# A Fourier mixer followed by hash routing: routing in two parts, scatters paced by stage 2, tables in three parts

## The chip, the cores and the metric

The kernel runs on one core of one Trainium2 chip. The metric is the device time of one execution in microseconds. A core has five engines with their own instruction streams: TensorE (PE; its weight loads are shown as PEld), VectorE (DVE), ScalarE (ACT), GpSimd (POOL) and SyncE (SP). Here SP and ACT start ordinary DMA transfers, and POOL starts transfers by descriptors made in software, above all indirect ones (scatter and gather by an index). Each engine runs its instructions in program order, so an instruction that waits holds up all behind it on that engine.

## What is computed

The input x has 8 batches of 2496 tokens with 256 channels. Each channel goes through a real Fourier transform over the tokens, is multiplied by a complex filter, and is transformed back. The result is read as 19968 tokens, and each token goes to one of eight experts, chosen by its id, which is a two-layer network with ReLU (256 to 1024 to 256):

```python
X = np.fft.rfft(x, axis=1)
y = np.fft.irfft(X * (filt_r + 1j * filt_i)[None], n=x.shape[1], axis=1)
x = y.reshape(B * S, D)
expert_idx = token_ids * np.int64(2654435761) % np.int64(E)
for e in range(E):
    mask = expert_idx == e
    out[mask] = np.maximum(x[mask] @ w1[e], 0.0) @ w2[e]
```

All arithmetic is in 32-bit floats.

## The kernel before

**The mixer.** The transform of length 2496 is done as 39 by 64. Per batch there are three stages. Stage 1 (`stage1`, PSUM tile pa) multiplies x tiles by a table of 39-point transforms; ACT copies the result to t1, and ACT's queue stores it to a DRAM buffer d1. Stage 2 (`stage2`, eleven steps: `forward` of step u and `back` of step u - 1) reads d1 in another layout as tiles t2 (`load2`, five loads per batch), multiplies by the table d_t (pb), applies the filter on DVE (y and z: four operations per step), multiplies by the transposed table e_t (pc), and stores through ACT to a DRAM buffer d2. Stage 3 (`stage3`, six pieces) reads d2 as tiles t4 (`load4`), multiplies by the inverse table (pd), copies to o and stores to `mixed` in DRAM (`store3`). For batches 0 and 1 the copy to o is on ACT, for the others on DVE. There are two buffers of o, two of t1, four of t2.

**The routing.** `count`, `route` and `places` (lines 407 to 495) work out on DVE, for every token, its row in `lists`, so that each expert's tokens fill tiles of 128. `listed` scatters token numbers into `lists` with indirect DMAs on POOL, 128 tokens each: 39 scatters for the tokens of each of the four routing stages (batches 0 and 1, 2 and 3, 4 and 5, 6 and 7). `blanks` computes the unused rows and marks them with 7 scatters more. `tile_experts` and `experts` work out which expert each of the 163 tiles belongs to.

**The tables.** `load_tables` loads d_t and the filter in two parts: entries 0 to 7 through SP, 8 to 19 through POOL as soon as the second x tile is there (line 358). `spread_filters` copies the filter to other partitions (DVE and ACT), and `way_back` transposes d_t into e_t on TensorE.

**The experts.** For each of 163 tiles: `load` reads a list (SP) and gathers its rows of mixed (POOL), `turn` transposes them on TensorE (xps, xt), `up` does the first layer (ups) and `down` the second (dps), and the result is scattered to the output (POOL). Weights are loaded when a tile's expert differs. `load` runs four tiles ahead. A tile of a routing stage may be gathered only when its two batches are mixed.

**The order** is written out by hand: `todo` (lines 583 to 605) is a list of pieces, each with a due time. Pieces below zero are issued first, in order of their times; the rest are issued between `up` and `down` of the expert tile whose number is their time. So the opening, before the first expert tile, holds stages 1 to 3 of batches 0 and 1, stage 1 of batch 2 and the first routing stage. A load's due time is put a few steps ahead of its use, but not before the argument `ready`.

Of the kernel before, what the change touches and what calls it, by code (L numbers as in the profile page):

```python
# [11 lines left out]
F32 = mybir.dt.float32  # L12
I32 = mybir.dt.int32
AF = mybir.ActivationFunctionType
OP = mybir.AluOpType
AX = mybir.AxisListType
# [3 lines left out]
P = 128  # L20
B, S, C = 8, 2496, 256
N = B * S
E, F = 8, 1024
# [6 lines left out]
NS, NQ = N1 // 2 + 1, 64  # L30
# [6 lines left out]
NU = (HN + XG) // XG  # L37
# [6 lines left out]
TB = 128  # L44
NT = (N + E * (TB - 1)) // TB
LW = 16
NJ = N // (4 * P)
DP = C // P
FP = F // P
STAGES = (2, 4, 6, 8)  # L50
G = len(STAGES)
NPAD = NT * TB - N
NQP = NPAD // P

# [53 lines left out]
def kernel(  # L108
# [39 lines left out]

    ident = keep.tile([P, P], F32)
    slots = keep.tile([P, G, NJ], I32)  # L150
    number = keep.tile([P, NJ, LW], I32)
    chunk_i = keep.tile([1, 2, NT], I32)
    wf_t = cpool.tile([NR, NK], F32)
# [5 lines left out]
    class Batch:  # L159
# [119 lines left out]
        def stage3(self, u):  # L279

            o = opool.tile([NR, XG, C], F32, name=f"o_{self.b}_{u}", tag="o")
            v, half = divmod(u, XL // XG)

            copy = nc.scalar.copy if self.b < 2 else nc.vector.tensor_copy
            self.products(wi_t, (NK, 2 * NS), N1, self.t4[v][:, half * XG:half * XG + XG, :], o, copy, u, "pd")

            last, self.o = self.o, (o, u)
            if last and self.b >= 2:
                self.store3(*last)
            if self.b < 2 or u == NU - 1:  # L290
                self.store3(o, u)

        def store3(self, o, u):
# [17 lines left out]
    def listed(g, j0, j1):  # L311

        if j0 == 0:
            nc.gpsimd.iota(number[:], pattern=[[1, NJ], [0, LW]], base=P * NJ * g, channel_multiplier=NJ)
        for j in range(j0, j1):
            scatter(number[:, j, :], slots[:, g, j:j + 1], f"lists_{g}")

    batches = [Batch(b) for b in range(B)]

# [28 lines left out]
    rt = rpool.tile([P, 2 + NQP], F32)  # L348
    nc.scalar.dma_start(out=rt[:], in_=r_dram.ap())

    S_PARTS = (slice(0, 8), slice(8, NS))

    def load_tables(part):
        sl = S_PARTS[part]
        eng = nc.sync if part == 0 else nc.gpsimd
        if part:

            nc.gpsimd.tensor_copy(junk[:], batches[0].x[1][0:1, 0, 0:1])
        eng.dma_start(out=d_t[:, sl, :], in_=d_dram.ap()[:, sl, :])
        for k in range(2):  # L360
            load_filter(k, sl, eng)
# [45 lines left out]
    def count():  # L407
# [1 line left out]
        eid_i = slots[:].rearrange("p g j -> p (g j)")  # L409
        nc.vector.tensor_scalar(eid_i, tok[:].rearrange("p g j two -> p (g j) two")[:, :, 0], E - 1, None,  # L410
                                op0=OP.bitwise_and)
        eid = rpool.tile([P, G * NJ], F32)
        nc.vector.tensor_copy(eid[:], eid_i)
        mask = rpool.tile([P, E, G * NJ], F32)
        nc.vector.tensor_tensor(mask[:], eid[:].unsqueeze(1).to_broadcast([P, E, G * NJ]),
                                iota_e[:].unsqueeze(2).to_broadcast([P, E, G * NJ]), op=OP.is_equal)
        maskf = mask[:].rearrange("p e j -> p (e j)")
        run = rpool.tile([P, E * G, NJ], F32)
# [14 lines left out]
    def route():  # L433
# [1 line left out]


        upto = rpool.tile([P, G, E], F32)
        made_in = ps[:, 0, 0:E * G].rearrange("p (e g) -> p g e", g=G)
        nc.vector.tensor_copy(upto[:, 0, :], made_in[:, 0, :])
        for g in range(1, G):  # L440
            nc.vector.tensor_tensor(upto[:, g, :], upto[:, g - 1, :], made_in[:, g, :], op=OP.add)
        full_i = rpool.tile([P, G, E], I32)
        nc.vector.tensor_copy(full_i[:], upto[:])
        nc.vector.tensor_scalar(full_i[:, G - 1, :], upto[:, G - 1, :], float(TB - 1), None, op0=OP.add)
# [27 lines left out]
        nc.vector.tensor_scalar(off0[:], off[:, 0, :], -1.0, None, op0=OP.add)  # L472
        thr = rpool.tile([P, G, E], F32)
        nc.vector.tensor_scalar(thr[:], full[:, 0:G, :], float(TB), 1.0, op0=OP.mult, op1=OP.add)
        acc = rpool.tile([P, E, G * NJ], F32)
        tmp = mask
        nc.vector.tensor_tensor(run[:], run[:], base[:].rearrange("p e g -> p (e g)").unsqueeze(2)
                                .to_broadcast([P, E * G, NJ]), op=OP.add)
        run = run[:].rearrange("p (e g) j -> p e (g j)", g=G)
        nc.vector.tensor_tensor(run, run, mask[:], op=OP.mult)  # L480
        for e in range(E):
            nc.vector.scalar_tensor_tensor(acc[:, e, :], mask[:, e, :], off0[:, e:e + 1], run[:, e, :],
                                           op0=OP.mult, op1=OP.add)
        for g in range(1, G):
            for e in range(E):
                nc.vector.tensor_scalar(tmp[:, e, :], run[:, e, :], thr[:, g, e:e + 1], step[:, g, e:e + 1],
                                        op0=OP.is_ge, op1=OP.mult)
            nc.vector.tensor_tensor(acc[:], acc[:], tmp[:], op=OP.add)

        rv.update(acc=acc, upto=upto, full_t=full_t, made=made, first=first, last=last)  # L490

    def places():
        slot = rv["eid"]
        nc.vector.tensor_reduce(slot[:], rv["acc"][:].rearrange("p e j -> p j e"), axis=AX.X, op=OP.add)
        nc.vector.tensor_copy(slots[:].rearrange("p g j -> p (g j)"), slot[:])

    def tile_experts():
        last = rv["last"]
# [13 lines left out]
    def blanks():  # L512
# [18 lines left out]
        nc.vector.tensor_tensor(at[:], at[:], index, op=OP.add)  # L531
        nc.vector.scalar_tensor_tensor(at[:], first[:, G - 1, 0:1].to_broadcast([P, NQP]), float(TB), at[:],
                                       op0=OP.mult, op1=OP.add)
        at_i = rpool.tile([P, NQP], I32)
        nc.vector.tensor_copy(at_i[:], at[:])
        blank = rpool.tile([P, LW], I32)
        nc.gpsimd.memset(blank[:], N)
        for q in range(NQP):
            scatter(blank[:], at_i[:, q:q + 1], "lists_pad")

    def experts():
        seg = rv["seg"]
# [14 lines left out]
    def spaced(t0, t1, n):  # L557
        return [t0 + (t1 - t0) * u / n for u in range(n)]
# [21 lines left out]
    N_2 = NS // 2 + 1  # L580


    todo = part1(0, spaced(-155, -143, NU)) + [(-152.5, count), (-152.4, route), (-152.3, places)]
    todo += [(-154.9, lambda: load_tables(0)), (-154.8, lambda: load_tables(1))]
    todo += [(t, lambda k=k: way_back(k)) for k, t in enumerate([-142.7, -142.5, -122, -121.8, -121.6])]
    todo += [(-141, lambda: spread_filters(0)), (-125, lambda: spread_filters(1))]
    todo += part2(0, spaced(-131, -101, N_2), -138)
    todo += part1(1, spaced(-129, -105, NU), [-150, -149, -136])
    todo += [(-140, tile_experts), (-130, experts), (-60, blanks)]
    todo += [(-142, lambda: listed(0, 0, NJ))]  # L590
    todo += [(-110, lambda: nc.sync.dma_start(out=wi_t[:], in_=wi_dram.ap()))]
    todo += [(-82 + .1 * i, lambda i=i: (weights(i, 0), weights(i, 1))) for i in range(2)]
    todo += part2(1, spaced(-100, -70, N_2), -103) + part3(0, spaced(-92, -73, NU), -97)
    todo += part1(2, spaced(-70, -60, NU), [-104, -103.9, -78]) + part3(1, spaced(-59.5, -48, NU), -66)

    todo += part1(3, spaced(2, 7, NU)) + part1(4, spaced(15, 20.5, NU))
    todo += part1(5, spaced(21, 27, NU)) + part1(6, spaced(36, 46, NU)) + part1(7, spaced(50, 60, NU))
    todo += part2(2, spaced(.1, 7.4, N_2), -40) + part2(3, spaced(8.5, 15.5, N_2), 7)
    todo += part2(4, spaced(22, 31, N_2), 20.5) + part2(5, spaced(31.2, 46, N_2), 28)
    todo += part2(6, spaced(48, 62, N_2), 47) + part2(7, spaced(63.2, 80, N_2), 61)  # L600
    todo += part3(2, spaced(8, 14, NU), 7.5) + part3(3, spaced(17, 25, NU), 15.6)
    todo += part3(4, spaced(33, 44, NU), 31.5) + part3(5, spaced(49, 63, NU), 46.5)
    todo += part3(6, spaced(67, 83, NU), 62) + part3(7, spaced(84, 101, NU), 81)
    for g, (t0, t1) in enumerate([(1, 23), (30, 62), (70, 102)]):
        todo += [(t, lambda g=g, j=j: listed(g + 1, j, j + 1)) for j, t in enumerate(spaced(t0, t1, NJ))]
    todo.sort(key=lambda t: t[0])
    pre = [t for t in todo if t[0] < 0]
    main = [t for t in todo if t[0] >= 0]
# [11 lines left out]
    def load(i):  # L620

        g = stage_of[i]
        if i % 2 == 0:
            n = min(2, NT - i)
            lst[i] = gath.tile([P, 2, LW], I32, name=f"lst_{i}", tag="lst")
            step = tiles[i + 1] - tiles[i] if n == 2 else 1
            ld = nc.sync.dma_start(
                out=lst[i][:, 0:n, :],
                in_=bass.AP(tensor=lists[:].tensor, offset=lists[:].offset + tiles[i] * TB * LW,
                            ap=[[LW, P], [step * TB * LW, n], [1, LW]]))  # L630
            for later in range(g + 1, G):
                tc.declare_no_dep(ld.ins, group=f"lists_{later}", reason="the tiles of a stage hold tokens of its batches alone")
            tc.add_to_no_dep_group("lists_read", ld.ins)
        xg[i] = gath.tile([P, C], F32, name=f"xg_{i}", tag="xg")
        rows = N + 1 if g == G - 1 else STAGES[g] * S
# [42 lines left out]
        tc.add_to_no_dep_group("out_rows", st.ins)  # L678
        del xg[i]

    for i in range(4):
        load(i)
    turn(0)
    for i in range(NT):
        ht = work.tile([P, FP, TB], F32, name=f"ht_{i}", tag="ht")
        if i + 4 < NT:
            load(i + 4)
        up(i, ht)
        weights(i + 2, 0)
        if i + 1 < NT:  # L690
            turn(i + 1)
        while main and main[0][0] < i + 1:
            main.pop(0)[1]()
        down(i, ht)
        weights(i + 2, 1)
# [29 lines left out]
```

## Time and profile before

| | |
|---|---|
| time | 1719.93 us, median of 3 runs (1709.46 to 1722.15) |
| span of the profiled execution | 1715.1 us |
| TensorE busy, granted clock | 1538.2 us, 0.947 |
| DVE, ACT, POOL busy | 534.9, 216.8, 508.9 us |
| moved by DMA | 257.70 MB, mean 150 GB/s |
| first expert matmul (line 658) | 247.67 us after the start |

The profile is one execution. Busy shares are means over the whole span; the opening of some 248 us and the rest have different limits, so the views by stretches of time are the ones to read. In a listing by time, a line gives start, duration, engine, line of the kernel, operation, tiles written and read, and in brackets how long the engine stood idle before and what ended that wait.

### The profile page before, as it was taken

To read this page: it belongs to the slowest core of one execution; us is meant where nothing else is said; L and a number is where in the kernel's file an instruction comes from. 1 tells how busy PE (TensorE), PEld (TensorE's weight loads), DVE (VectorE), ACT (ScalarE), POOL (GpSimd) and SP (SyncE) were. 2 spreads that over 40 slices of the span, in tenths; PEclk is the share of its full clock that TensorE was granted. 3 is DMA by queue.
4 is the path that set the end of the run, shared out by engine and by line. 5 is a ranking of instruction groups with operands and counts; after the bars stand their busy time and mean duration, and the time that the engine had idled before them with its cause. 6 is when DMAs were issued, how large, how long until landed. Compare 5 with 4: busy or idle time off the path is not lost.

```text
span 1715.1 us, 27107 instructions
## 1 busy us (share of the span) xinstructions
PE 1538.2 (90%) x9522; PEld 1388.9 (81%) x9522; DVE 534.9 (31%) x970; ACT 216.8 (13%) x371; POOL 508.9 (30%) x515
## 2 busy tenths in 40 slices
PE   3266659989997999999999999999999999999997
PEld 2154438867886899989888999899899999999997
DVE  6155104345223444423332444122222122221121
ACT  2031211101111111111110101000000000000000
POOL 2710113322322133433333233344332222222221
PEclk7577769989998999999999999999999999999999
DMA  8378555665766488366554664443426222222220
GB/s 240 111 239 228 149 169 158 196 156 166 209 193 191 126 261 254 112 200 168 148 190 127 191 203 135 128 146 85 158 64 210 88 88 87 87 86 85 85 81 12
DMA packets 160868, 257.70 MB, mean 150 GB/s; under 512 B 38817, under 2 KB 121412, under 8 KB 158733
## 3 DMA queue, kind: packets, MB, share of 16 engines
q1 hardware_dynamic: 102833, 143.67, 28.1%
q10 hardware_dynamic: 35484, 62.57, 11.7%
q0 software_dynamic: 22416, 49.74, 9.5%
q8 instruction: 76, 1.25, 0.3%
q14 instruction: 59, 0.48, 0.1%
HBM read 431.77 MB, written 85.09 MB: 301 GB/s over the span
## 4 chain that ended last, share of the span: by engine, by line
PE 82%; DMA 7%; issue 4%; DVE 3%; another core or an unknown queue 2%; ACT 1%; SPq 1%; ACTq 0%; POOL 0%; POOLq 0%; DVEq 0%
PE ups L658 33%; PE dps L670 32%; PE pd L198 4%; PE pc L258 4%; PE pa L198 4%; PE pb L235 3%; DMA d<-t 2%; DMA t<-d 2%; PE xps L647 2%; DVE z L245 1%; DMA mixed<-o 1%; DMA d<-g 1%; DVE y L242 1%; PE pd L193 0%
## 5 line engine op out<-in xcount | busy, mean ns | idle before, releaser
L658 PEld LDWEIGHTS ups<-xt,w 128*128 128x128 f32 x5216 | 610.8, 193 | 9.4 <-DVE xt L649 1.1
L658 PE MATMUL ups<-xt,w 128*128 128x128 f32 x5216 | 611.6, 276 | 0.7 <-DVE xt L649 0.7
L670 PE MATMUL dps<-w,ht 128*128 128x256 f32 x2608 | 596.6, 382 | 5.8 <-DMA w<-in_moe_w_dram 4.7
L670 PEld LDWEIGHTS dps<-w,ht 128*128 128x128 f32 x2608 | 492.6, 192 | 73.1 <-DMA w<-in_moe_w_dram 5.1
L674 POOL DMA_INDIRECT out_dram<-osb,lst x163 | 161.8, 993 | 628.3 <-DVE osb L673 603.7
L636 POOL DMA_INDIRECT xg<-mixed,lst x163 | 173.3, 1063 | 387.7 <-DMA lst<-lists 140.1
L664 DVE TENSOR_SCALAR ht<-ups 128x512 f32<-128x512 f32 x163 | 112.8, 692 | 556.2 <-PE ups L658 422.3
L662 ACT ACTIVATE ht<-ups 128x512 f32<-128x512 f32 x163 | 97.3, 597 | 1042.4 <-PE ups L658 602.8
L673 DVE COPY osb<-dps 128x256 f32<-128x256 f32 x163 | 69.2, 425 | 399.7 <-PE dps L670 392.8
L304 POOL DMA_INDIRECT lists<-number,slots x156 | 155.6, 997 | 72.2 <-issue 47.0
L258 PE MATMUL pc<-y,e_t 128*128 128x256 f32 x320 | 92.3, 414 | 49.6 <-DVE z L245 28.2
L258 PEld LDWEIGHTS pc<-y,e_t 128*128 128x128 f32 x320 | 63.5, 205 | 67.9 <-issue 53.2
L245 DVE TENSOR_TENSOR z<-pb,filt 64x512 f32<-64x512 f32 x160 | 110.2, 689 | 2.2
L235 PE MATMUL pb<-t,d_t 128*128 128x256 f32 x320 | 89.6, 406 | 20.2 <-DMA t<-d 17.7
L198 PE MATMUL pd<-t,wi_t 120*117 120x256 f32 x320 | 87.9, 422 | 17.2 <-DMA t<-d 7.6
L242 DVE TENSOR_TENSOR y<-pb,filt 128x512 f32<-128x512 f32 x80 | 55.2, 690 | 113.8 <-PE pb L235 62.6
L198 PEld LDWEIGHTS pd<-t,wi_t 120*117 120x117 f32 x320 | 62.2, 203 | 33.9 <-ACT o L200 6.1
L235 PEld LDWEIGHTS pb<-t,d_t 128*128 128x128 f32 x320 | 61.8, 203 | 33.4 <-issue 22.5
L649 DVE COPY xt<-xps 128x256 f32<-128x256 f32 x163 | 67.7, 415 | 57.9 <-PE xps L647 56.5
L261 ACT COPY g<-pc 128x512 f32<-128x512 f32 x80 | 46.7, 586 | 258.1 <-PE pc L258 175.0
L198 PE MATMUL pa<-x,wf_t 117*120 117x256 f32 x264 | 64.9, 393 | 7.2 <-DMA x<-in_x_dram 7.2
L647 PE MATMUL xps<-ident,xg 128*128 128x128 f32 x326 | 62.5, 274 | 7.1 <-DMA xg<-mixed,lst 7.1
(102 smaller groups left out, 390.5 us busy)
## 6 DMA issues: line engine op xcount, KB each, us to landing
w<-in_moe_w_dram SPq DMA_DIRECT2D x322, 1024.0 KB
t<-d SPq DMA_DIRECT2D x80, 256.0 KB
d<-g ACTq DMA_DIRECT2D x80, 256.0 KB
mixed<-o ACTq DMA_DIRECT2D x120, 156.0 KB
d<-t ACTq DMA_DIRECT2D x16, 960.0 KB
t<-d SPq DMA_DIRECT2D x16, 960.0 KB
x<-in_x_dram SPq DMA_DIRECT2D x39, 312.0 KB
x<-in_x_dram SPq DMA_DIRECT2D x21, 234.0 KB
```

The lines of the kernel that those rows point to most:

```text
L198: nc.tensor.matmul(out=ps[0:cols * H, k, :], lhsT=w[:], rhs=src[:, 2 * i + k, :], start=True, stop=True)
L235: nc.tensor.matmul(out=ps[:, i, :], lhsT=d_t[:, s, :], rhs=self.t2[s // SG][:, s % SG, :], start=True, stop=True)
L245: nc.vector.tensor_tensor(out=z[b], in0=ps[a], in1=f_t[1][a, sl, :], op=OP.mult)
L258: nc.tensor.matmul(out=ps[:, i, :], lhsT=e_t[:, 2 * u + i, :], rhs=pr[:, i, :], start=True, stop=True)
L304: st = nc.gpsimd.indirect_dma_start(out=lists[:], out_offset=bass.IndirectOffsetOnAxis(ap=index, axis=0), in_=rows, in_offset=None, bounds ...
L636: ld = nc.gpsimd.indirect_dma_start(out=xg[i][:], out_offset=None, in_=mixed[0:rows, :], in_offset=bass.IndirectOffsetOnAxis(ap=lst[i // 2 ...
L647: nc.tensor.transpose(out=ps[:, dp, :], in_=xg[i][:, dp * P:(dp + 1) * P], identity=ident[:])
L658: nc.tensor.matmul(out=ps[:, k, :], lhsT=w1[:, dp, fp * P:(fp + 1) * P], rhs=xt[i][:, dp, :], start=(dp == 0), stop=(dp == DP - 1))
L662: nc.scalar.activation(out=dst, in_=ps[:], func=AF.Relu)
L664: nc.vector.tensor_scalar_max(dst, ps[:], 0.0)
L670: nc.tensor.matmul(out=ps[:], lhsT=ht[:, fp, :], rhs=w2[:, fp, :], start=(fp == 0), stop=(fp == FP - 1))
L674: st = nc.gpsimd.indirect_dma_start(out=out[:], out_offset=bass.IndirectOffsetOnAxis(ap=lst[i // 2 * 2][:, i % 2, 0:1], axis=0), in_=o[:], ...
```

## The change

It works on the opening, and a little on the expert part.

- The routing is done in two parts. `places(0, 1)` works out the rows of the first routing stage alone, before stage 2 of batch 0; `places(1, G)` does the other three after stage 2 of batch 1. Operations over single experts become operations over all eight.
- The 39 scatters of the first routing stage are issued in pairs, one pair after each step of stage 2 of batches 0 and 1. Each pair reads its rows from a tile `place`, into which DVE copies them at that point of its own order, so that a pair can't start before DVE has come there.
- The tables are loaded in three parts: entries 0 to 7 and 8 to 11 through SP at the start, 12 to 19 through POOL once the first t2 tile of batch 0 is there (`behind`).
- The x loads of batch 1 are placed between the t2 loads of batch 0, and stage 1 of batch 1 runs in the second half of stage 2 of batch 0.
- In stage 3 of batches 0 and 1, a piece's store is issued after the next piece's copies, as for the other batches.
- The seven scatters of blanks move to the times of expert tiles 62 to 69. Some due times in the expert part change a little. Near the end of a routing stage, `load` runs two tiles ahead instead of four.

The diff, cut to its core:

```diff
-            if last and self.b >= 2:
+            if last:
                 self.store3(*last)
-            if self.b < 2 or u == NU - 1:
+            if u == NU - 1:
                 self.store3(o, u)
...
+        index = slots[:, g, :]
+        if g == 0:
+            nc.vector.tensor_copy(place[:, j0:j1], index[:, j0:j1])
+            index = place
         for j in range(j0, j1):
-            scatter(number[:, j, :], slots[:, g, j:j + 1], f"lists_{g}")
+            scatter(number[:, j, :], index[:, j:j + 1], f"lists_{g}")
...
-    S_PARTS = (slice(0, 8), slice(8, NS))
+    S_PARTS = (slice(0, 8), slice(8, 12), slice(12, NS))
+    def behind(ap):
+        nc.gpsimd.tensor_copy(junk[:], ap)
     def load_tables(part):
-        eng = nc.sync if part == 0 else nc.gpsimd
-        if part:
-            nc.gpsimd.tensor_copy(junk[:], batches[0].x[1][0:1, 0, 0:1])
+        eng = nc.sync if part < 2 else nc.gpsimd
...
+    def places(g0, g1):
+        nc.vector.tensor_tensor(run, run, rv["base"][:, :, g0:g1].unsqueeze(3).to_broadcast([P, E, n, NJ]), op=OP.add)
+        nc.vector.tensor_tensor(run, run, mask, op=OP.mult)
+        nc.vector.tensor_tensor(acc, mask, each(rv["off"][:]), op=OP.mult)
+        nc.vector.tensor_tensor(acc, acc, run, op=OP.add)
         for g in range(1, G):
-            for e in range(E):
-                nc.vector.tensor_scalar(tmp[:, e, :], run[:, e, :], thr[:, g, e:e + 1], step[:, g, e:e + 1],
-                                        op0=OP.is_ge, op1=OP.mult)
-            nc.vector.tensor_tensor(acc[:], acc[:], tmp[:], op=OP.add)
+            nc.vector.tensor_tensor(mask, run, each(rv["thr"][:, g, :]), op=OP.is_ge)
+            nc.vector.tensor_tensor(mask, mask, each(rv["step"][:, g, :]), op=OP.mult)
+            nc.vector.tensor_tensor(acc, acc, mask, op=OP.add)
...
-    todo = part1(0, spaced(-155, -143, NU)) + [(-152.5, count), (-152.4, route), (-152.3, places)]
+    todo = part1(0, spaced(-155, -143, NU)) + [(-152.5, count), (-152.4, route), (-142.95, lambda: places(0, 1))]
     todo += [(-154.9, lambda: load_tables(0)), (-154.8, lambda: load_tables(1))]
-    todo += part2(0, spaced(-131, -101, N_2), -138)
-    todo += part1(1, spaced(-129, -105, NU), [-150, -149, -136])
-    todo += [(-140, tile_experts), (-130, experts), (-60, blanks)]
-    todo += [(-142, lambda: listed(0, 0, NJ))]
+    todo += [(-129, lambda: behind(first.t2[0][0:1, 0, 0:1])), (-128.9, lambda: load_tables(2))]
+    todo += [(-140, tile_experts), (-139.9, experts), (-65, lambda: places(1, G)), (-64.9, blanks)]
+    todo += part2(0, spaced(-127, -97, N_2), -138) + part1(1, spaced(-113, -97, NU), [-128, -122, -116])
-    todo += [(-82 + .1 * i, lambda i=i: (weights(i, 0), weights(i, 1))) for i in range(2)]
-    todo += part2(1, spaced(-100, -70, N_2), -103) + part3(0, spaced(-92, -73, NU), -97)
-    todo += part1(2, spaced(-70, -60, NU), [-104, -103.9, -78]) + part3(1, spaced(-59.5, -48, NU), -66)
+    todo += part2(1, spaced(-96, -66, N_2), -96.5) + part3(0, spaced(-87, -70, NU), -96.4)
+    todo += [(t + .1, lambda j=j: listed(0, 2 * j, min(2 * j + 2, NJ)))
+             for j, t in enumerate((spaced(-127, -97, N_2) + spaced(-96, -66, N_2))[:NJ // 2 + 1])]
+    todo += [(-79 + 3 * i, lambda i=i: (weights(i, 0), weights(i, 1))) for i in range(2)]
+    todo += part1(2, spaced(-65, -56, NU), [-80, -78, -62]) + part3(1, spaced(-55, -45, NU), -64)
-    todo += part3(2, spaced(8, 14, NU), 7.5) + part3(3, spaced(17, 25, NU), 15.6)
+    for b, t1, t2, t3 in [(2, None, (.1, 8), (9.9, 14.5)), (3, (2, 7), (8.5, 16), (18, 25)),
...
+    todo += [(t, lambda q=q: padded(q)) for q, t in enumerate(spaced(62, 69, NQP))]
...
-        if i + 4 < NT:
-            load(i + 4)
+        while loaded < NT and loaded <= i + (4 if stage_of[loaded] == stage_of[min(i + 2, NT - 1)] else 2):
+            load(loaded)
+            loaded += 1
```

## The prediction

> **What bounds the kernel now.** I read the page's busy shares and slices first, then the table by stretches of time, then the time-ordered listing of the opening and the chain.
>
> ```profile
> PE 1538.2 (90%) x9522; PEld 1388.9 (81%) x9522; DVE 534.9 (31%) x970; ACT 216.8 (13%) x371; POOL 508.9 (30%) x515
> PE   3266659989997999999999999999999999999997
> PEclk7577769989998999999999999999999999999999
> DMA  8378555665766488366554664443426222222220
> PE 82%; DMA 7%; issue 4%; DVE 3%; another core or an unknown queue 2%; ACT 1%; SPq 1%; ACTq 0%; POOL 0%; POOLq 0%; DVEq 0%
> ```
>
> TensorE is full from the seventh slice on (a slice is 43 us). The idle time, 1715 - 1538 = 177 us, is mostly in the first six slices. By stretches (columns: length, then busy time and instruction count of PE, PEld, DVE, ACT, POOL, then granted clock, DMA share, GB/s):
>
> ```profile
> 25.00:50.00 25.00, 2.97 (x10) 1.78 (x10) 13.71 (x27) 4.99 (x7) 9.85 (x10) 0.50 0.85 255
> 50.00:75.00 25.00, 9.04 (x28) 5.98 (x28) 3.88 (x9) 1.17 (x2) 19.03 (x20) 0.64 0.27 79
> 75.00:100.00 25.00, 9.06 (x20) 5.63 (x20) 9.25 (x12) 5.44 (x6) 13.24 (x15) 0.57 0.52 170
> 200.00:225.00 25.00, 13.64 (x44) 9.98 (x44) 0.00 (x0) 4.05 (x8) 0.24 (x1) 0.80 0.95 252
> 225.00:250.00 25.00, 9.02 (x25) 5.66 (x26) 0.42 (x1) 3.96 (x8) 5.12 (x5) 0.53 0.55 183
> ```
>
> From 0 to 50 us the DMA engines are the limit (0.85, 255 GB/s). From 50 to 100 us nothing is: every compute engine and the DMA are mostly idle and only POOL works. The listing of that stretch:
>
> ```profile
> 34.35 1.07 ACT L200 COPY t<-pa 120x512 f32<-120x512 f32 x2 [15.57 <-DMA d<-t]
> 36.30 0.24 DVE L495 CAST slots<-eid 128x156 int32<-128x156 f32 x1
> 50.18 2.04 PE L235 MATMUL pb<-t,d_t 128*128 128x256 f32 x4 [11.46 <-DMA t<-d]
> 67.38 0.58 ACT L200 COPY t<-pa 120x512 f32<-120x512 f32 x1 [9.22 <-remote]
> 67.42 0.98 POOL L304 DMA_INDIRECT lists<-number,slots  x1 [0.30 <-issue]
> 78.58 0.69 DVE L242 TENSOR_TENSOR y<-pb,filt 128x512 f32<-128x512 f32 x1 [22.28 <-issue]
> 89.83 0.58 ACT L261 COPY g<-pc 128x512 f32<-128x512 f32 x1 [21.87 <-remote]
> ```
>
> pa for the copy at 67.38 was issued by 56.4, pb for the multiply at 78.58 by 57.2, pc for the copy at 89.83 by 59.3; yet ACT and DVE start 11, 21 and 30 us later, on no releaser that the profile can name. All this falls inside an unbroken run of 39 scatters on POOL, one per 1.285 us from 37.4 to 87.7, and the last hold ends 2 us after that run. The same shows once more, smaller, at 484.9 to 488.5 us, after five indirect DMAs in a row on POOL. Against it: seven scatters in a row from 191 to 200 held nobody. So that a run of indirect DMAs holds the hand-over from TensorE is a correlation, not a proof.
>
> The first expert matmul (ups) starts at 247.67 us; from there 163 tiles take 1467 us, of which TensorE is idle 51 us by the gaps between its matmuls, and that stretch holds the same work in both kernels. So the question is when the first ups starts.
>
> **What the Trainium skill says.** "DMA: Bandwidth & Descriptors", section "Issuing engines are not separate DMA queues": transfers started by SP, ACT and POOL share the same 16 engines and interleave. The trace agrees: the d1 store issued at 13.99 takes 20.3 us while tables come in from two queues, and the one issued at 36.87, alone, 5.4 us. "VectorE: DVE Perf Modes", section "The TRN2 errata": a fixed cost per instruction of about 150 cycles; the trace has 0.69 us for 512 elements and 1.46 for 1248, hence 1.04 ns an element and 0.16 us fixed, which fits. "TensorE: Matmul & The Clock Gate", Part 1: the clock is full or half by recent activity. Here it is 0.50 to 0.64 in the idle stretches, so removing idle also shortens the matmuls after it. No page that I found says that indirect DMAs hold TensorE's signals.
>
> **The change, part by part.**
>
> *Tables in three parts.* POOL's early load was 768 KB of d_t and four times 384 KB of filter, 2.3 MB. One third goes to SP at once, two thirds (1.54 MB) wait behind the first t2 tile. At the 255 GB/s of the second stretch 1.54 MB are 6 us. The d1 store that released ACT at 34.35 should land near 28, and the last d1 store of batch 0 (42.3 now) near 35.
>
> *x of batch 1 between stage 2's loads.* On SP six x loads of 312 KB stood ahead of the first t2 load, 1.87 MB, 7 us at 255 GB/s; part of it fell into the dip at 35 to 40 us, so I count 6. Together: first pb at 38 instead of 50.2. The price: stage 1 of batch 1 moves to the end of stage 2 of batch 0, so its last d1 store falls behind the ninth forward step.
>
> *Routing in two parts.* Before, L477 to the slots' cast: 17.2 to 36.5 us. After, 13 operations on a quarter (312 elements): 0.16 + 0.33 = 0.48 us each, 6.2, a reduce of 0.7 and a cast of 0.2: 7.1 us, slots of stage 0 at 24.3. No longer near the path; DVE then waits for DMA anyway. The other three quarters: 13 at 0.16 + 936 x 1.04 = 1.13, 14.7, plus 2: 17 us after stage 2 of batch 1, where DVE has no work (0.00 from 200 to 225). Hidden.
>
> *Scatters two at a time.* Each pair follows a small DVE copy (place): 20 copies at some 0.2 us (0.17 to 0.24 for the small rows), 4 us of DVE in two stage 2s; in the first, where DVE sets the step, 2 us. POOL gets gaps between pairs: 2.6 us of scatter per step of 3.5 us. So no 50 us run exists. Whether the holds vanish with it is the unknown: from nothing saved to the whole 30 us (59.3 to 89.8). I take nearly all.
>
> From first pb of batch 0 to first pb of batch 1: now 50.2 to 136.0, 86 us. After: the undisturbed steps of this stage went at 3.5 us (six from 105.9 to 126.9), nine are 32; from the ninth forward to batch 1's first pb now 124.7 to 136, with one more step for stage 1's shift and d1's 6.8 and t2's 4.7 us: 17. Sum 49, first pb of batch 1 at 87, 49 us earlier. DMA in that time: 2.6 MB each of t2, x, d2, d1 and 1.5 of tables, 12 MB, 47 us at 255: just carried.
>
> *Stage 2 of batch 1 with stage 3 of batch 0*, now 136 to 190.6, 55 us at 171 GB/s. The 4 MB of first weights and 1.9 MB of x of batch 2 now fall here: 9.4 + 5.9 = 15.3 MB, 60 us at 255. It ends at 147.
>
> *Stores of stage 3 one piece later* (batches 0 and 1, on ACT, two o buffers). Queued behind: the copies of piece u + 2 need the buffer whose store has only just been issued, so ACT waits for a whole landing (2 to 5 us in the listing of 225 to 238) instead of part of one, and TensorE waits for PSUM behind it. In batch 0 other work lies beside it; for batch 1 four to five pieces at 1.5 us: 7 us. Bounds 0 and 15.
>
> *Stage 1 of batch 2, stage 3 of batch 1, first gather*: 190.6 to 247.7 now, 57 us, the same chain (x of batch 2 waits for its buffer, then d2, mixed, gather), plus 7: 64. First ups at 147 + 64 = 211 against 247.7: 37 us.
>
> *Main part.* Stage 3 of batch 2 starts at 9.9 instead of 8 tiles; the gap of 5.9 us at tile 9 (waiting for t4) should go. The seven blank scatters move to tiles 62 to 69, where POOL is busy a third of the time. Loads only two tiles ahead at a stage's border: lst and gather need some 6 us and a tile takes 9, hidden, at worst a few us at each of three borders. Net 4 us saved, bounds -10 and +10.
>
> Sum: 1719.9 - 37 - 4 = 1679, say 1680.
>
> **Rivals.** (1) *The holds are not the scatters' doing* and come back when stage 2 starts: 30 us returned, 1709. For it: the seven scatters that held nobody. Against: the end of the holds with the run, and the second case after five in a row. (2) *DMA becomes the bound* of the opening, at 230 GB/s instead of 255, with late stores costing ACT 15: the two stage-2 parts become 5 and 7 us longer and the tail 8, so 1700. For it: first 50 us at 0.85 share. (3) *Slower*: the delayed stores, the border loads and the shifted stage 1 together cost more than the opening gains: holds return (30), stores at 15 (8 more), borders at +10 (14 more): 1680 + 52 = 1732. It needs all the bad ends at once.
>
> **How the numbers follow.** Forecast 0.66, rival 1 0.14, rival 2 0.14, rival 3 0.06. 1% is 17 us, that is 1703 and 1737. Rival 2 lies on that edge, half counted faster: faster 0.73; rival 1, the other half and most of rival 3 within 1%: 0.23; slower by more 0.04. The range goes from 1652 (late stores free, tables and x worth 8 us more, main part at its good end) to 1714, which holds rivals 1 and 2.
>
> **What would show it.** First pb near 38 us; slots' first cast near 24; no ACT or DVE wait over 5 us without a named releaser in stage 2 of batch 0; POOL's scatters with gaps; first pb of batch 1 near 87; first ups near 211. Wrong if waits of 10 to 20 us without releaser stay, if ACT's waits on mixed stores exceed 15 us in stage 3 of batch 1, or if new TensorE gaps stand at tiles 30, 70 and 108.

## The result and the profile after

The changed kernel takes 1669.59 us (median of 4 runs, 1662.86 to 1676.55), the kernel before 1719.20 in the same comparison (4 runs, 1709.46 to 1722.15): a ratio of 0.9721, with an interval of 0.9665 to 0.9778. The forecast was 1680; the step that it rested on, the earlier first ups, was forecast at 211 us and came at 214.2. The kernel before took about 1720 us here, but about 1675 in two later jobs; the section on the experiments takes that up.

The page of the changed kernel, its busy shares, slices (42 us each) and chain by engine:

```profile
PE 1527.5 (92%) x9522; PEld 1380.8 (83%) x9522; DVE 541.4 (32%) x982; ACT 216.9 (13%) x372; POOL 508.9 (31%) x515
PE   4755489899889999999999999999999999999997
PEclk8986689999999999999999999999999999999999
DMA  8886725756674784485646644544253323222220
PE 82%; DMA 8%; issue 4%; DVE 3%; another core or an unknown queue 1%; ACTq 1%; ACT 1%; POOL 0%; SPq 0%; POOLq 0%; DVEq 0%
```

TensorE is full from the sixth slice on instead of the seventh. Its work is the same (9522 matmuls) and its busy time 10.7 us less; the mean granted clock is 0.961 against 0.947.

The table by stretches of time of the changed kernel (columns as in the prediction):

```profile
25.00:50.00 25.00, 14.01 (x50) 9.35 (x50) 15.08 (x32) 8.14 (x12) 9.77 (x12) 0.75 0.83 227
50.00:75.00 25.00, 19.25 (x81) 15.29 (x82) 16.51 (x29) 10.31 (x17) 11.65 (x12) 0.93 0.75 236
...
225.00:250.00 25.00, 25.00 (x142) 22.48 (x141) 11.04 (x19) 5.29 (x9) 8.88 (x9) 0.93 0.39 127
```

The empty stretch from 50 to 75 us is gone: 81 matmuls instead of 28, 29 DVE operations instead of 9, DMA share 0.75 instead of 0.27. From 225 to 250 us TensorE has no gap; before, that stretch was a third full.

The listing by time of the changed kernel, cut to the points that the prediction named:

```profile
25.75 0.18 DVE L510 CAST slots<-tok 128x39 int32<-128x39 f32 x1
...
36.59 3.75 PE L238 MATMUL pb<-t,d_t 128*128 128x256 f32 x8 [6.27 <-DMA t<-d]
...
41.45 0.16 DVE L321 COPY place<-slots 128x2 int32<-128x2 int32 x1
42.46 1.06 POOL L307 DMA_INDIRECT lists<-number,place  x1 [2.69 <-DVE place L321]
...
91.12 3.75 PE L238 MATMUL pb<-t,d_t 128*128 128x256 f32 x8 [8.86 <-DMA t<-d]
...
120.60 0.58 ACT L203 COPY o<-pd 117x512 f32<-117x512 f32 x1 [6.24 <-DMA mixed<-o]
...
1253.11 0.66 PE L661 MATMUL xps<-ident,xg 128*128 128x128 f32 x2 [3.12 <-DMA xg<-mixed,lst]
```

In order: the rows of the first routing stage, the start of stage 2 of batch 0, the first `place` copy and its scatter, the start of stage 2 of batch 1, a copy of a late-stored piece, and a gather at a stage's border. In stage 2 of batch 0, the longest wait of ACT or DVE on no named releaser is 1.2 us.

| start of | before | forecast | after |
|---|---|---|---|
| first pb of batch 0 | 50.2 | 38 | 36.6 |
| first pb of batch 1 | 136.0 | 87 | 91.1 |
| last pb of batch 1 | 185.1 | | 146.2 |
| end of stage 2 of batch 1 (next pa) | 190.6 | 147 | 151.7 |
| first ups (tile 0) | 247.7 | 211 | 214.2 |
| ups of tile 30 | 617.3 | | 566.2 |
| ups of tile 108 | 1306.8 | | 1258.3 |
| end of span | 1715.1 | | 1666.5 |

The opening gave 33.5 us and the expert part another 15: the lead over the kernel before grows to 51.1 us at tile 25, is 53.3 at tile 100, and falls to 48.5 at tile 108, where the last line of the listing stands.

### The profile page after: what moved, and what is told of

The parts are those of the page before. It is cut to its first block, busy times and chain, and to the rows that moved or that the text cites. A ratio compares the mean times of both kernels' runs of the same rounds, so it can differ in the third digit from the quotient of the medians.

```text
span 1666.5 us, 27145 instructions
## 1 busy us (share of the span) xinstructions
PE 1527.5 (92%) x9522; PEld 1380.8 (83%) x9522; DVE 541.4 (32%) x982; ACT 216.9 (13%) x372; POOL 508.9 (31%) x515
## 4 chain that ended last, share of the span: by engine, by line
PE 82%; DMA 8%; issue 4%; DVE 3%; another core or an unknown queue 1%; ACTq 1%; ACT 1%; POOL 0%; SPq 0%; POOLq 0%; DVEq 0%
PE dps L684 32%; PE ups L672 32%; PE pa L201 4%; DMA mixed<-o 4%; PE pc L261 4%; PE pb L238 3%; PE pd L201 3%; PE xps L661 2%; DVE z L248 1%; DMA d<-t 1%; DMA x<-in_x_dram 1%; DMA d<-g 1%; ACTq L299 1%; DVE y L245 1%
## 5 line engine op out<-in xcount | busy, mean ns | idle before, releaser
L307 POOL DMA_INDIRECT lists<-number,slots x117 | 117.0, 1000 | 37.5 <-issue 36.6
L261 PE MATMUL pc<-y,e_t 128*128 128x256 f32 x320 | 87.6, 398 | 26.7 <-DVE y L249 10.6
L201 PE MATMUL pd<-t,wi_t 120*117 120x256 f32 x320 | 83.9, 407 | 13.7 <-ACT o L203 11.5
L238 PEld LDWEIGHTS pb<-t,d_t 128*128 128x128 f32 x320 | 61.4, 202 | 27.9 <-issue 19.5
```

What stands on the lines that cost most here:

```text
L201: nc.tensor.matmul(out=ps[0:cols * H, k, :], lhsT=w[:], rhs=src[:, 2 * i + k, :], start=True, stop=True)
L238: nc.tensor.matmul(out=ps[:, i, :], lhsT=d_t[:, s, :], rhs=self.t2[s // SG][:, s % SG, :], start=True, stop=True)
L261: nc.tensor.matmul(out=ps[:, i, :], lhsT=e_t[:, 2 * u + i, :], rhs=pr[:, i, :], start=True, stop=True)
L307: st = nc.gpsimd.indirect_dma_start(out=lists[:], out_offset=bass.IndirectOffsetOnAxis(ap=index, axis=0), in_=rows, in_offset=None, bounds ...
```

## Experiments

They ran in three jobs, and the kernel before did not take the same time in them: 1721.39 us (1719.34 to 1726.41) in job A (labels e1 to e4), but 1675.01 (1672.38 to 1675.49) in job B (e5 to e8) and 1675.68 (1672.22 to 1681.75) in job C (f1 to f4). The first comparison (1719.20) looks like job A. So times are compared within a job, and ratios to before across jobs only with care. Each kernel has one profile, of one execution.

What differs in the profiles is the very thing under study, the holds: ACT or DVE starts late although TensorE has long ended what it waits for. They can be counted in the expert part, where every tile hands two results of its first layer (ups) to ACT and to DVE (ht), 326 hand-overs in a profile. The delay is taken from the end of the last ups matmul, or from the end of the engine's own work before it if that is later. The table sorts the hand-overs by how many indirect DMAs POOL had started in a row (each less than 0.45 us after the end of the one before) when that matmul ended:

| in a row on POOL | first comparison and job A, six profiles | over 1 us late | jobs B and C, eight profiles | over 1 us late |
|---|---|---|---|---|
| 0 to 2 | 1648 | 0 | 2208 | 0 |
| 3 | 200 | 22 | 275 | 0 |
| 4 | 40 | 35 | 52 | 0 |
| 5 or more | 68 | 66 | 73 | 0 |

So in the first six profiles, 17 to 26 hand-overs of each are late (by up to 5.9 us), all of them when at least three DMAs had started in a row, and 118 of the 123 end within 2 us of the run's end. In the other eight no hand-over is late by more than 0.5 us, at the same kind of runs. The condition lies outside the program. The record lists jobs A and B under the same chip number and job C under another, so that number doesn't sort the two conditions.

### e1_run39 (job A): the 39 scatters again in one run

The pairs are replaced by one run right after the first step of stage 2 of batch 0; all else stays changed. The theory was that the run holds TensorE's hand-over to ACT and DVE; the rival, that the holds of the kernel before had another cause that the rest of the change removed.

```diff
-    todo += [(t + .1, lambda j=j: listed(0, 2 * j, min(2 * j + 2, NJ)))
-             for j, t in enumerate((spaced(-127, -97, N_2) + spaced(-96, -66, N_2))[:NJ // 2 + 1])]
+    todo += [(-126.9, lambda: listed(0, 0, NJ))]
```

> The changed kernel, but all 39 scatters of the first routing stage are issued in one run on POOL from the first step of stage 2 of batch 0, after one copy of all their rows. Theory (a run of indirect DMAs holds TensorE's signals): waits of ACT and DVE of 10 to 20 us on no named releaser come back inside the run, from about 43 to 93 us, and the first expert matmul is 15 to 35 us later than the 214 us of the changed kernel; time 1685 to 1705. Rival (the holds had another cause, such as the order of the loads): no such waits, first expert matmul within 4 us of 214, time 1670.

Measured: 1699.29 us (1683.92 to 1708.77), ratio 0.9843 (0.9781 to 0.9904), against 0.9721 of the whole change. First pb of batch 1 at 123.4, first ups at 239.2; the two kernels of the same job that keep the pairs and undo one load order (e3, e4 below) have 99.0 and 95.8, 217.3 and 217.9. The listing by time of this kernel:

```profile
77.69 0.58 ACT L203 COPY t<-pa 120x512 f32<-120x512 f32 x1 [5.08 <-remote]
...
95.36 0.69 DVE L245 TENSOR_TENSOR y<-pb,filt 128x512 f32<-128x512 f32 x1 [26.63 <-remote]
...
96.86 0.98 POOL L307 DMA_INDIRECT lists<-number,place  x1 [0.30 <-issue]
...
102.42 0.58 ACT L264 COPY g<-pc 128x512 f32<-128x512 f32 x1 [17.06 <-remote]
```

The holds are back, now while the tables, x loads and routing stand as in the changed kernel, and the last one ends some 5 us after the run's last scatter (96.86). TensorE had ended the pb of the multiply at 95.36 by 70.9 and the pc of the last copy by 73.8, so these two start 24 and 29 us late. The first ups is 21 to 22 us later than in e3 and e4, which have pairs, and 25 later than in the changed kernel's profile. So under this job's condition the unbroken run brings the long holds of the opening, and pairing removes them. The rival falls, for this condition. The times alone would not show it: e1's four executions spread from 1684 to 1709, the profile is of the slowest, and its interval overlaps those of e3 and e4.

### e2_stores_now, e3_tables_early, e4_x_early (job A): one part undone each

e2 stores each piece of stage 3 of batches 0 and 1 right after its copies, as before:

```diff
-            if last:
+            if last and self.b >= 2:
                 self.store3(*last)
-            if u == NU - 1:
+            if self.b < 2 or u == NU - 1:
                 self.store3(o, u)
```

> The changed kernel, but in stage 3 of batches 0 and 1 each store follows its own copies, as before. Theory (the later stores cost 7 us in stage 3 of batch 1 because the buffer of o comes free a landing later): first expert matmul at about 207 instead of 214 us and time 1663. Rival (DMA is what limits there, so the order of the stores is hidden): within 2 us of 214, time 1670.

Measured: 1662.37 us (1653.07 to 1669.26), ratio 0.9653 (0.9609 to 0.9697). Last pb of batch 1 at 133.1 and first ups at 192.3, 13 and 22 us earlier than in the changed kernel's profile. The first ups was expected at 207. Of the 22 us, 6 are left at the end (span 1660.9 against 1666.5): from the first ups on e2 takes 1468.6 us and the changed kernel 1452.3, with 22 late hand-overs against 17. The late stores cost the opening time; this pair of profiles is of different jobs, so f4 measures the size.

e3 loads the second and third part of the tables together, through POOL behind the second x tile, as before:

```diff
-    S_PARTS = (slice(0, 8), slice(8, 12), slice(12, NS))
+    S_PARTS = (slice(0, 8), slice(8, NS))
...
-        eng = nc.sync if part < 2 else nc.gpsimd
+        eng = nc.sync if part < 1 else nc.gpsimd
...
-    todo += [(-154.9, lambda: load_tables(0)), (-154.8, lambda: load_tables(1))]
-    todo += [(-129, lambda: behind(first.t2[0][0:1, 0, 0:1])), (-128.9, lambda: load_tables(2))]
+    todo += [(-154.9, lambda: load_tables(0)), (-154.85, lambda: behind(first.x[1][0:1, 0, 0:1])), (-154.8, lambda: load_tables(1))]
...
```

> The changed kernel, but the tables in two parts as before: entries 8 to 19 through POOL as soon as the second x tile is there. Theory (1.5 MB ahead of the d1 stores at 255 GB/s): first pb at 42 to 43 instead of 36.6 us, of which a part is given back since DMA has 1.5 MB less to carry in stage 2 of batch 0; first expert matmul at 214 to 220, time 1670 to 1676. Rival (only the hold mattered, DMA catches up): first pb later but first expert matmul within 2 us of 214.

e4 loads x of batch 1 ahead of all t2, as before:

```diff
-    todo += part2(0, spaced(-127, -97, N_2), -138) + part1(1, spaced(-113, -97, NU), [-128, -122, -116])
+    todo += part2(0, spaced(-127, -97, N_2), -138) + part1(1, spaced(-113, -97, NU), [-150, -149, -136])
```

> The changed kernel, but the x loads of batch 1 stand ahead of the first t2 loads on SP, as before. Theory (1.9 MB ahead of the first t2 load): first pb at 42 to 44 instead of 36.6 us; x is then no longer to be carried in stage 2 of batch 0, so a part comes back: first expert matmul at 214 to 220, time 1670 to 1676. Rival (bytes are only moved about): first expert matmul within 2 us of 214.

Measured: e3 1683.71 us, ratio 0.9791 (0.9772 to 0.9811); e4 1681.19, 0.9770 (0.9738 to 0.9803). Each has its first pb at 44.5 us, between the 50.2 of before and the 36.6 of the changed kernel: one of the two moves alone brings 5.7 us, the second 7.9 more. At the first ups (217.3 and 217.9 against 214.2) only 3 to 4 of the 7.9 are left. In e4 some of it comes back in stage 2 of batch 0, which then has no x of batch 1 to load (51.3 us from its first pb to that of batch 1, against 54.5). In e3 that stage takes 54.6, and what comes back comes after the last pb of batch 1 (64.3 us to the first ups, against 68.0), for a reason that isn't shown. The totals lie above the expected 1670 to 1676; that they are 0.5 to 0.7% above the changed kernel's ratio is about the width of the intervals.

### e5_iotas, e6_runs13 (job B), f2_iotas (job C): which property of the run holds

e5 and f2 put 130 iotas on POOL in place of the run, work without DMAs, and scatter later in fours. e6 splits the run in three of 13.

```diff
...
+    todo += [(-126.9, busy)]
+    todo += [(t + .1, lambda j=j: listed(0, 4 * j, min(4 * j + 4, NJ))) for j, t in enumerate(spaced(-96, -56, 10))]
```

```diff
+    todo += [(-126.9, lambda: listed(0, 0, 13)), (-107.8, lambda: listed(0, 13, 26)), (-90.4, lambda: listed(0, 26, NJ))]
```

> The changed kernel, but POOL runs 130 iotas without a gap (some 40 us, into a tile that nobody reads) from the first step of stage 2 of batch 0, and the 39 scatters follow in ten groups of four during stage 2 of batch 1 and after. Theory A (it is the run of indirect DMAs that holds TensorE's signals): no wait of ACT or DVE over 5 us on no named releaser while the iotas run; first pb of batch 1 at 91 us as in the changed kernel, first expert matmul at 212 to 218. Theory B (any unbroken work on POOL holds them): waits of 10 us and more during the iotas, first pb of batch 1 at 105 us or later.

> The changed kernel, but the scatters of the first routing stage in three runs of 13 (17 us each) with gaps of 10 us or more between them. Theory A with a threshold (the run of 39 held signals only from its fifteenth to twentieth scatter on): no holds, first pb of batch 1 near 91 us, time 1665 to 1676. Rival (each run holds from its start): waits without a named releaser in each run, first pb of batch 1 at 100 us or later, time 1680 to 1700.

> The kernel of e5 again (130 iotas on POOL in place of the run of scatters), on the chip of f1. Where f1 shows holds: theory A (indirect DMAs are needed) expects none here and the first expert matmul within 6 us of the changed kernel's, theory B (any unbroken work on POOL) expects waits of 10 us and more. Where f1 shows none, none here either, and this run tells nothing.

Measured, one time each: 1644.87, 1644.91 and 1648.12 us. None has a hold. But no profile of jobs B and C has one, so these three say nothing on what property of the run matters. They are inconclusive.

### e7_before_pairs (job B): the kernel before with pairs alone

```diff
+        if g == 0:
+            nc.vector.tensor_copy(place[:, j0:j1], index[:, j0:j1])
+            index = place
...
-    todo += [(-142, lambda: listed(0, 0, NJ))]
+    todo += [(t + .1, lambda j=j: listed(0, 2 * j, min(2 * j + 2, NJ)))
+             for j, t in enumerate((spaced(-131, -101, N_2) + spaced(-100, -70, N_2))[:NJ // 2 + 1])]
```

> The kernel before with one part of the change alone: scatters of the first routing stage in pairs after the steps of stage 2 of batches 0 and 1, all due times as before. Theory (the holds cost 30 us of the opening and go with the run): first expert matmul at 215 to 225 instead of 248 us, time 1688 to 1700. Rival (the later bound takes most of it back): first expert matmul at 235 to 245, time 1706 to 1716.

Measured: 1662.05 us (1660.92 to 1664.29), ratio 0.9922 (0.9906 to 0.9939), 13 us, where 20 to 32 were hoped for at the slower condition; the first ups is at 211.9. There is no profile of the kernel before from this job, so it isn't shown what these 13 us are made of.

### f1_run39 and f3_after (job C): e1 and the changed kernel again, in one job

> The kernel of e1 again (one run of 39 scatters), to tell whether the chip matters: the kernel before took 1721 us in the job of e1 to e4 and 1675 in that of e5 to e8. Theory C (holds of TensorE's signals by a run of indirect DMAs happen on some chips only): where the kernel before takes about 1720 us, waits of 10 us and more on no named releaser and a time 25 to 40 us over the changed kernel; where it takes about 1675, no such wait, first expert matmul within 4 us of the changed kernel's. Rival (the two jobs differed in something else, and the run of 39 holds everywhere): the waits are there on either chip.

> The changed kernel itself beside the others. Where the kernel before takes about 1720 us: 1670, ratio 0.972. Where it takes about 1675, the change has no holds to take away, and what is left is the earlier opening (pairs alone gave 13 us there, the rest of the change some 18, four tiles ahead 7 of which this kernel lacks): 1648 to 1655, ratio 0.984 to 0.988.

Measured: f1 1644.31 us (1635.85 to 1654.79), ratio 0.9820 (0.9770 to 0.9870); f3, the changed kernel itself, 1637.51 (1636.12 to 1645.41), ratio 0.9778 (0.9746 to 0.9809). The two can't be told apart by time. f3 is faster than the 1648 to 1655 that were expected. The listing of f1, in the middle of its unbroken run of scatters (55 to 97 us):

```profile
67.53 0.58 ACT L203 COPY t<-pa 120x512 f32<-120x512 f32 x1 [1.17 <-PE pa L201]
...
70.12 0.58 ACT L264 COPY g<-pc 128x512 f32<-128x512 f32 x1 [1.14 <-PE pc L261]
```

The same program as e1, the same run on POOL, but ACT's waits here, from 65 to 75 us, all end with TensorE's result and are 0.3 to 1.2 us long. First pb of batch 1 is at 88.7 (e1: 123.4), first ups at 210.4, within the expected 4 us of f3's 207.3. So the unbroken run does not bring holds by itself: a condition that this execution lacks must be there too. Two of f1's four executions took 14 to 17 us longer (1651 and 1655) than the profiled one (1637.5); what they lost isn't known.

A short case in the expert part shows the same in the changed kernel alone. Its listing from 314 us, with seven indirect DMAs in a row on POOL since 312.57:

```profile
314.34 3.73 PE L672 MATMUL ups<-xt,w 128*128 128x128 f32 x32
...
320.50 0.99 POOL L307 DMA_INDIRECT lists<-number,slots  x1 [0.30 <-issue]
...
322.92 0.69 DVE L678 TENSOR_SCALAR ht<-ups 128x512 f32<-128x512 f32 x1 [7.96 <-remote]
...
326.82 2.05 PE L261 MATMUL pc<-y,e_t 128*128 128x256 f32 x4 [5.94 <-DVE y L249]
```

and of f3, the same program, the same tile, the last of the same seven and the same matmul:

```profile
305.65 3.73 PE L672 MATMUL ups<-xt,w 128*128 128x128 f32 x32
309.50 0.69 DVE L678 TENSOR_SCALAR ht<-ups 128x512 f32<-128x512 f32 x1 [3.22 <-PE ups L672]
...
311.91 0.99 POOL L307 DMA_INDIRECT lists<-number,slots  x1 [0.30 <-issue]
...
313.48 1.10 PE L261 MATMUL pc<-y,e_t 128*128 128x256 f32 x4 [1.28 <-DVE y L249]
```

In the first, DVE starts 4.9 us after the last ups (318.07) and TensorE stands for 5.94 us behind it; in the second DVE starts 0.1 us after it and TensorE waits 1.28.

So the changed kernel is not free of holds. Pairing took the long ones out of the opening, but the runs of DMAs in the expert part stayed: from the first ups to the end it takes 1452.3 us in the first comparison and 1427.3 in f3, and TensorE's waits there add up to 33.6 and 18.9 us.

f3 against e7 says what the rest of the change brings where nothing is held: 24.5 us by the medians (two jobs whose kernel before agrees within 0.7 us); e8 below, which is the changed kernel but for the stages' borders and ran in e7's job, gives 18.2. First ups differ by only 4.6 us (207.3 and 211.9), which is no more than two profiles of one opening can differ (f3 207.3, e8 212.4). The rest lies in tiles 0 to 30: 333.8 us in f3, 359.6 in e7. TensorE's waits in that stretch, by line (total, times, longest), of e7:

```profile
PE pc L259 <- DVE y L247: 11.5, 9, 2.1
PE pd L199 <- DMA t<-d: 5.9, 1, 5.9
PE dps L676 <- DMA w<-in_moe_w_dram: 4.2, 1, 4.2
```

and of f3:

```profile
PE pc L261 <- DVE y L249: 4.6, 3, 2.1
PE pd L196 <- DVE o L198: 4.1, 2, 2.1
```

All waits there add up to 28.6 us in e7 and 11.7 in f3: 17 of the 26 us. The wait for t4 (pd on t) and the one for weights are gone, and stage 2 of later batches waits for DVE three times instead of nine. Which due time does which of these wasn't tried alone. The other 9 us are TensorE's busy time, 331.5 us in e7 and 322.8 in f3 for the same work, at a mean granted clock of 0.964 and 0.988.

### e8_ahead4 (job B): loads four tiles ahead at the borders too

```diff
-        while loaded < NT and loaded <= i + (4 if stage_of[loaded] == stage_of[min(i + 2, NT - 1)] else 2):
+        while loaded < NT and loaded <= i + 4:
```

> The changed kernel, but load runs four tiles ahead everywhere, also at the end of a routing stage. Theory (two tiles ahead is too late at tile 108, where TensorE waits 3 us for the gather, and costs 5 us there): that gap goes, tile 108 comes 50 to 53 us earlier than before instead of 48.5, time 1665. Rival (four ahead makes POOL wait for mixed at the borders of tiles 30 and 70 and its other work queues behind): gaps of 3 us or more before those tiles, time 1672 to 1680.

Measured: 1643.87 us (1642.67 to 1647.07), ratio 0.9822 (0.9805 to 0.9838). The gap at tile 108 is gone, and tiles 60 to 108 take 389.5 us instead of 391.8 in f3. At tiles 30 and 70 neither kernel has a gap. The border costs some 2 us, too little to be seen in the total, which is above f3's in the other job.

### f4_both (job C): stores at once and four ahead

The edits of e2 and e8 together.

> The changed kernel with two edits: stores of stage 3 of batches 0 and 1 right after their copies (e2) and load four tiles ahead everywhere (e8). Theory (late stores cost 8 us and more in the opening, late loads 7 us at tile 108, and the two add up): 14 to 25 us faster than the changed kernel in this job, first expert matmul near 192. Rival (what the stores give in the opening is lost again in the expert part, as it was in part in e2): 5 to 10 us faster.

Measured: 1624.56 us (1623.33 to 1626.34, 5 runs), ratio 0.9688 (0.9667 to 0.9709), 12.9 us below f3 in the same job. This is the fastest kernel of the study; the gain lies between the 14 to 25 us of the theory and the rival's 5 to 10. First ups is at 196.5 (f3: 207.3), 10.8 us earlier, and up to there only the stores differ. Of the 10.8, 2.0 are there at the first pb of batch 1 (87.4 and 89.4), before any of these stores, and aren't explained; 7.3 come in stage 2 of batch 1 with stage 3 of batch 0 beside it (47.5 us from the first to the last pb, against 54.8); 1.5 come after it. The 7.3 us are firm: e8, whose opening is the same program as f3's, takes 54.9 for that stage. The 1.5 are not: what follows takes 63.1 us in f3, 61.6 in f4 and 66.7 in e8. ACT's waits between 85 and 215 us that end on a store to mixed add up to 41.6 us in f3 and 9.9 in f4. Some 32 us less of waiting on ACT are worth 9 to 11 us at the first ups: the length of a wait is not its price. The price shows at TensorE, which waits in stage 3's own matmuls (pd) until ACT has copied o. In stage 2 of batch 1, of f3:

```profile
119.04 1.25 PE L201 MATMUL pd<-t,wi_t 120*117 120x256 f32 x4 [3.18 <-ACT o L203]
...
129.78 2.06 PE L201 MATMUL pd<-t,wi_t 120*117 120x256 f32 x4 [1.75 <-ACT o L203]
...
141.70 1.07 PE L196 MATMUL pd<-t,wi_t 40*39 40x256 f32 x2 [4.08 <-ACT o L198]
```

and of f4:

```profile
132.47 1.07 PE L196 MATMUL pd<-t,wi_t 40*39 40x256 f32 x2 [1.50 <-ACT o L198]
```

These add up to 9.0 and 1.5 us, and the difference is about the 7.3 us of the stage.

## Why the prediction was right, and where it was not

**The opening's start: right.** Slots cast at 25.75 (24.3 worked out from 0.16 us plus 1.04 ns an element), first pb at 36.6 (38). "VectorE: DVE Perf Modes" of the Trainium skill, section "The TRN2 errata", holds at the new sizes: 0.48 us for 312 elements and 1.13 for 936, both as forecast. The 12 us were put together from 6 for the tables and 6 for x; e3 and e4 bear that out, 5.7 for the first of the two and 7.9 for the second, whichever comes first. One reading of the trace there is weaker than it looks: the d1 stores of 20.3 and 5.4 us are of 960 and 600 KB, so size makes a part of the difference.

**The holds: right under its condition, and the reason too narrow.** "Up to 30 us, taken nearly whole" became 32 us at the first pb of batch 1 and 25 at the first ups (e1 against the changed kernel's profile; 24 to 28 and 21 to 22 against e3 and e4 of its own job). The prediction argued from a correlation: an unbroken run on POOL, then late starts of ACT and DVE. e1 turns it into a cause, in job A. f1 adds what no single profile could show: under another condition the same run held nobody in the profiled execution, and there the change still gains 38 us (1675.68 to 1637.51). So the forecast's main term isn't the only thing that carries the result: the gain is 49.6 us in the first comparison and 38.2 in job C. Nor did the holds show only "once more" in the kernel before: 18 hand-overs of its expert part are late, and 17 in the changed kernel, which the prediction counted for nothing on either side.

**The first ups: errors that partly cancel.** First pb came 1.4 us early, from there to the first pb of batch 1 it took 54.5 us instead of 49, then 60.6 instead of 60 and 62.5 instead of 64. The 5.5 us are the largest miss of the opening. Nine steps took 33.1 us (32 forecast); from the ninth forward step to batch 1's first pb it took 21.4 (17 forecast).

**Stage 2 of batch 1 with stage 3 of batch 0: the right length for a wrong reason.** It began at 91.1 (87) and ended at 151.7 (147), 60.6 us for the 60 of the forecast, which was 15.3 MB at 255 GB/s. Bytes and rate came as forecast, 15.6 MB at 257 GB/s. But f4 has the same loads at the same due times and moves its 15.5 MB in 53.0 us. The same stretch of the changed kernel and of f4 (columns as in the prediction):

```profile
91.10:151.70 60.60, 38.90 (x125) 27.34 (x126) 30.27 (x51) 11.47 (x21) 20.35 (x22) 0.75 0.82 257
87.40:140.40 53.00, 38.66 (x125) 28.05 (x126) 30.27 (x51) 11.47 (x21) 20.37 (x22) 0.79 0.90 292
```

So 255 GB/s was not the floor of this stage; TensorE's waits for ACT behind the late stores were. With the stores at once the DMA share is 0.90, and DMA may well be what limits next.

**Late stores: the size near, the place wrong.** Forecast: 7 us in batch 1's stage 3, nothing in batch 0's, where "other work lies beside it". The sign that would show it wrong did come: ACT's waits on mixed stores in batch 1's stage 3 add up to 19.5 us, more than the 15 named. Yet by f4 against f3 these cost 1.5 us, no more than two profiles differ by (18.6 us of such waits in f3), while those of batch 0, 23.0 us in f3 and in the changed kernel's first profile and one of them the 6.24 in the listing above, cost 7.3: together 8.8, near the 7 and by luck. In batch 0 the other work is not beside the wait but behind it: TensorE waits in pd for ACT's copy of o, and the pb and pc of stage 2 come after that pd in its program order. In batch 1's stage 3 TensorE waits for ACT's o copies too, 14.6 us in f3, but in f4 11.1 us of waits in pd are still there, 5.5 of them for a store itself. In the first condition the stores may cost more: e2 takes 45.7 and 59.2 us for the same two stretches, the changed kernel of the first comparison 55.1 and 68.0, but these are profiles of different jobs. The forecast asked what work lies beside the wait, and not in whose queue.

**The expert part: right in sign, mis-sized.** Forecast 4 us saved within -10 and +10; it was 15 in the first pair of profiles. The named term (the 5.9 us at tile 9) did go, by f3 against e7, but the prediction priced only that: it left out DVE's late y (7 us of waits fewer) and the weights (5). In the first pair, a hold that cost TensorE 5.94 us at tile 10 took the place of the removed wait at tile 9.

**Borders: "hidden, at worst a few us".** One gap of 3.12 us at tile 108 (2.17 in f3), none at tiles 30 and 70.

**The rivals.** Rival 1, that the holds have another cause, falls by e1 where holds exist. DMA as the bound (rival 2) did not come as a whole: its share from 50 to 75 us is 0.75 and TensorE is busy 19 of 25 us there. But its first part did in size: stage 2 of batch 0 came out 5.5 us longer than forecast, at 225 GB/s (share 0.79), and no run tells whether DMA is the reason. Of rival 3 only the stores came near its price.

**What stays open.** What makes the condition in which TensorE's signals come late, and whether it is a run of DMAs, their descriptors or any unbroken POOL work that does it there. The three kernels made for it met the other condition. Nor is the length of the run all: in the kernel before, the seven scatters from 191 us held nobody, and DVE started at 52.26 without delay on the first pb, while POOL was at its twelfth scatter of the run. Nor is it shown that holds are the whole of the 46 us by which the kernel before differs between jobs; there is no profile of it from jobs B and C.

## What to carry to other kernels

A start of ACT or DVE that is late on a finished matmul, with no releaser in the profile, is worth setting against what POOL does at the time. Breaking a long run of indirect DMAs with small dependent steps costs little (0.16 us of DVE a pair here) and took 25 us of delay out of the opening where there were holds; short runs, of four or five, are worth looking for as well. A wait for a store costs what stands behind it in program order, on the engine that waits and on the one that needs its result: the same delay of stores cost 7 us where TensorE had another stage's matmuls behind the wait, and under 2 in the next stage, where other waits took its place. And before crediting a part of a change, run the kernel before in the same job: here it moved by 2.7% between jobs, as much as the change itself.

## What the runs showed of the hardware

Between jobs, the same program has either late starts of ACT and DVE on finished results of TensorE (in e1 24 us on one DVE multiply and 29 on an ACT copy) or none (f1). In the expert part of the six profiles that have them, a hand-over was late by over 1 us in 66 of 68 cases when five or more indirect DMAs had started in a row on POOL, in 35 of 40 at four, 22 of 200 at three, and in none of 1648 below; in the eight profiles of jobs B and C in none of 2608. POOL itself ran at the same pace in both conditions, one scatter per 1.285 us (median of e1 and of f1).
